# Token blocks of 512, split weights kept in DRAM, attention by pairs of heads, two element-wise steps as parametric ReLU on ScalarE

## The chip, the cores and the metric

One core of one Trainium2 chip. The metric is the device time of one execution in microseconds (us). Engines are named as in the profile: PE is TensorE's matmul side, PEld its weight loads, DVE VectorE, ACT ScalarE, POOL GpSimd, SP the SyncE queue that issues every DMA here.

## What is computed

Linear attention with random features over 4 batches of 8 heads, 576 tokens and 64 channels, and behind it two feed-forward layers on the 2304 tokens by 512 channels that come out of it:

```python
def phi(x):
    proj = np.einsum('bhsd,df->bhsf', x, w_phi)
    proj = proj - np.max(np.abs(proj), axis=-1, keepdims=True)
    return np.concatenate([np.exp(proj), np.exp(-proj)], axis=-1)
q_p, k_p = (phi(q), phi(k))
kv = np.einsum('bhsf,bhsd->bhfd', k_p, v)
z = np.sum(k_p, axis=2)
num = np.einsum('bhsf,bhfd->bhsd', q_p, kv)
den = np.einsum('bhsf,bhf->bhs', q_p, z)[..., None] + 1e-06
x = (num / den) laid out as 2304 x 512
h = x @ w_in;  x = np.maximum(0.01 * h, h) @ w_out     # layer 0, 512 -> 2048 -> 512
h = x @ w_in2; r = np.maximum(h, 0.0); out = (r * r) @ w_out2   # layer 1
```

The weights of the two layers are handed over as float64 words.

## The kernel before

**Split products.** Each float32 operand of the layers is split into a high part (rounded to float32r) and a low part (the rest, again float32r), and a product is three float32r matmuls: high x high, high x low, low x high. `copy` (line 256 on ACT, 258 on DVE) makes high parts, `sub` (line 261, DVE) low parts, so one line stands for many steps and the tiles' names tell them apart. All matmuls are issued at line 252.

**The two layers.** The hidden dimension is 16 chunks of 128. Layer 0 takes the tokens in 8 blocks of 288 (`HALF`), layer 1 in 6 blocks of 384 (`BLK2`). For a block and a chunk, `moe` issues the h part (12 matmuls, moving tiles `xh`, `xl` of the block against the chunk's `wih`, `wil`, into bank 74 or 75 in turn), the activation (`a` on ACT, `g` on DVE, high part `gh`, low part `gl`), and some chunks later the y part, which sums over the chunks in banks of its own. In layer 0 the activation is a copy scaled by 0.01 on ACT (L433) and a maximum on DVE (L441); in layer 1 a ReLU on ACT (L435) and a square on DVE (L443). Layer 0's y goes to DRAM (`x2d`), and layer 1 reads it back and splits it (`x2h`, `x2l`).

**The weights.** `w_fetch` loads a half chunk (w_in or w_out, 512 KB of float64 words, `raw`) and converts it: ACT scales the upper words (L347), DVE mends the sign (L352), shifts the lower words (L356) and joins both into `wf` (L361). Then `w_load` splits `wf` into the high and low part of one of 9 ring slots. The ring does not hold 16 chunks, so blocks go through the chunks forwards and backwards in turn; what must come again is kept as the 256 KB of `wf` in DRAM (`wsd`), and after each reload split again.

**Attention.** `k_pair` makes, for two heads, phi(k) and the sums over tokens (`kp`, `kvh`, `kvl`); `q_pair` makes phi(q) for two heads and 288 tokens (POOL's all-reduce for the maximum, `qm`, `qe`), the products, the reciprocal (L775), the product with it, and the block's `xh`, `xl`. Batch 0 is done in plain float32 (its matmuls show as two records each), batches 1 to 3 in split form (`qs`, `qeh`, `qel`). `i` counts the 8 stretches of 288 tokens, two per batch.

**The order.** A planner (`Plan.order`) gives every operation a position and a cost and writes one fixed order per engine; engines run their queues in that order. While it waits at the start, PE is given filler matmuls on a tile of zeros. SP's queue is in this order too, so a load that waits for a free buffer holds the ones behind it.

## Time and profile before

| | |
|---|---|
| three runs | 1041.18, 1042.75, 1045.9 us; median 1042.75 |
| the profiled execution | 1043.8 us, 1.8 above its span |
| its span | 1042.0 us |
| granted TensorE clock, mean | 0.987 |
| busy | PE 97%, PEld 92%, DVE 72%, ACT 58%, POOL 7% |
| DMA | 127.26 MB, mean 122 GB/s |

The span runs from the first instruction to the last. A matmul's recorded length overlaps the next one's, so PE's own pace is read from the starts of successive matmuls in a timeline, not from the mean length; for DVE and ACT the groups of instructions give a mean length each, and a window's busy time counts overlaps once.

### The profile page before, as it was taken

The numbers are of one execution on the slowest core, as the hardware profiler recorded it, in microseconds if no ns is written. First come the engines' busy times: TensorE is split into PE (matmuls) and PEld (weight loads), VectorE is DVE, ScalarE is ACT, GpSimd is POOL, SyncE is SP. The second block draws the span as 40 slices with busy tenths as digits, with TensorE's granted clock in tenths as the row PEclk, the third lists the DMA queues.
The fourth block names the chain that finished last, engine by engine and source line by source line (L and its number), as shares of the span: only waits on it lengthen the run. The fifth ranks groups of instructions, "written<-read, shape, count | busy, mean of one in ns | idle before, by whom it ended". The sixth has DMA issues, their size and how long they took to land.

```text
span 1042.0 us, 17543 instructions
## 1 busy us (share of the span) xinstructions
PE 1015.4 (97%) x6576; PEld 953.5 (92%) x6576; DVE 754.7 (72%) x1388; ACT 607.0 (58%) x1388; POOL 73.7 (7%) x37
## 2 busy tenths in 40 slices
PE   9986998999999999999999999999999999999998
PEld 7775998999999999999999999989999999999997
DVE  6999999988969989788896799985345263352442
ACT  5866777867657667567685566655344253342432
POOL 1210001111001110100110000000000000000000
PEclk9986999999999999999999999999999999999999
DMA  7577668413314314124032688875123032130300
GB/s 221 175 216 217 202 191 251 138 51 122 114 30 145 98 58 134 59 67 134 24 95 73 224 221 267 233 233 160 41 96 107 1 113 59 52 111 11 96 17 31
DMA packets 62566, 127.26 MB, mean 122 GB/s; under 512 B 6800, under 2 KB 15120, under 8 KB 62480
## 3 DMA queue, kind: packets, MB, share of 16 engines
q1 hardware_dynamic: 62480, 126.13, 40.0%
q8 instruction: 51, 0.84, 0.3%
q14 instruction: 35, 0.29, 0.1%
HBM read 101.99 MB, written 24.12 MB: 121 GB/s over the span
## 4 chain that ended last, share of the span: by engine, by line
PE 85%; DVE 7%; DMA 3%; ACT 3%; issue 1%; SPq 0%; DVEq 0%; ACTq 0%
PE bank L252 85%; DMA raw<-wd 2%; DVE wf L361 1%; DVE qden L775 1%; DVE raw L356 1%; DVE raw L352 1%; DVE wol L261 1%; DVE qs L261 1%; DMA x2d<-y 1%; DMA wsd<-wf 1%; DVE wil L261 0%; ACT raw L347 0%; DMA kt<-kd 0%; ACT qden L763 0%; DVE kmx L598 0%
## 5 line engine op out<-in xcount | busy, mean ns | idle before, releaser
L252 PE MATMUL bank<-xh,wih 128*128 128x288 f32 x512 | 153.3, 300 | 0.7 <-DVE g L441 0.3
L252 PE MATMUL bank<-xh,wil 128*128 128x288 f32 x512 | 151.4, 296 | 2.6 <-DVE wil L261 2.6
L261 DVE TENSOR_TENSOR gl<-g,gh 128x288 fp32r<-128x288 f32 (+1 forms) x224 | 115.1, 515 | 53.0 <-ACT gh L256 52.3
L256 ACT ACTIVATE gh<-g 128x288 fp32r<-128x288 f32 (+1 forms) x224 | 106.0, 475 | 80.4 <-DVE g L443 55.3
L252 PE MATMUL bank<-gh,woh 128*128 128x288 f32 x512 | 152.6, 298 | 0.0
L252 PE MATMUL bank<-gl,woh 128*128 128x288 f32 x512 | 151.3, 296 | 1.1 <-DVE gl L261 1.0
L252 PE MATMUL bank<-xl,wih 128*128 128x288 f32 x512 | 151.2, 295 | 0.0
L252 PE MATMUL bank<-gh,wol 128*128 128x288 f32 x512 | 150.7, 294 | 0.0
L252 PE MATMUL bank<-x2h,wil 128*128 128x384 f32 x384 | 130.1, 339 | 0.5 <-DVE wil L261 0.5
L252 PE MATMUL bank<-x2l,wih 128*128 128x384 f32 x384 | 130.5, 340 | 0.0
L252 PE MATMUL bank<-x2h,wih 128*128 128x384 f32 x384 | 129.1, 336 | 1.3 <-ACT wih L256 1.3
L252 PE MATMUL bank<-woh,gl 128*128 128x512 f32 x288 | 114.4, 397 | 0.0
L252 PE MATMUL bank<-wol,gh 128*128 128x512 f32 x288 | 114.0, 396 | 0.0
L443 DVE TENSOR_TENSOR g<-a 128x384 f32<-128x384 f32 x96 | 53.3, 555 | 83.4 <-ACT a L435 83.3
L252 PE MATMUL bank<-woh,gh 128*128 128x512 f32 x288 | 112.4, 390 | 0.1
L261 DVE TENSOR_TENSOR wol<-wf,woh 128x512 fp32r<-128x512 f32 x116 | 79.4, 686 | 42.3 <-ACT woh L256 41.7
L707 POOL PARTITION_ALL_REDUCE qm<-qps x32 | 73.2, 2287 | 478.5 <-ACT qps L256 236.0
L435 ACT ACTIVATE a<-bank 128x384 f32<-128x384 f32 x96 | 46.5, 484 | 96.2 <-PE bank L252 96.2
L256 ACT ACTIVATE woh<-wf 128x512 fp32r<-128x512 f32 x111 | 69.6, 628 | 52.2 <-PE bank L252 46.6
L252 PEld LDWEIGHTS bank<-xh,wil 128*128 128x128 f32 x512 | 96.6, 189 | 3.1 <-DVE wil L261 3.1
L252 PEld LDWEIGHTS bank<-xh,wih 128*128 128x128 f32 x512 | 96.8, 189 | 2.1 <-DVE g L441 1.3
L252 PEld LDWEIGHTS bank<-gl,woh 128*128 128x128 f32 x512 | 96.1, 188 | 2.0 <-DVE gl L261 1.7
(94 smaller groups left out, 2195.8 us busy)
## 6 DMA issues: line engine op xcount, KB each, us to landing
wf<-wsd SPq DMA_DIRECT2D x168, 256.0 KB, 2.8
raw<-wd SPq DMA_DIRECT2D x64, 512.0 KB, 4.6
wsd<-wf SPq DMA_DIRECT2D x56, 256.0 KB, 4.8
qt<-qd SPq DMA_DIRECT2D x32, 288.0 KB, 2.9
vt<-vd SPq DMA_DIRECT2D x16, 325.0 KB, 3.3
x2d<-y SPq DMA_DIRECT2D x32, 144.0 KB, 2.4
x2s<-x2d SPq DMA_DIRECT2D x6, 768.0 KB, 5.0
out<-o SPq DMA_DIRECT2D x18, 256.0 KB, 2.5
```

The source lines that it names most:

```text
L252: nc.tensor.matmul(out=o, lhsT=lhsT, rhs=rhs, start=start, stop=stop, **kw)
L256: nc.scalar.activation(out=out, in_=in_, func=ACTF.Copy)
L261: ENG[e].tensor_tensor(out=out, in0=a, in1=b, op=ALU.subtract)
L352: nc.vector.scalar_tensor_tensor(out=hf, in0=hf, scalar=2.0 ** 32, in1=hf, op0=ALU.mult, op1=ALU.min)
L356: nc.vector.tensor_scalar(out=low, in0=low, scalar1=29, scalar2=None, op0=ALU.logical_shift_right)
L361: nc.vector.scalar_tensor_tensor(out=t["f"].bitcast(I32), in0=high, scalar=3, in1=low, op0=ALU.logical_shift_left, op1=ALU.bitwise_or)
L435: nc.scalar.activation(out=t["a"], in_=o, func=ACTF.Relu)
L443: nc.vector.tensor_tensor(out=t["g"], in0=t["a"], in1=t["a"], op=ALU.mult)
L707: nc.gpsimd.partition_all_reduce(out_ap=t["m"].rearrange("p h s -> p (h s)"), in_ap=t["ps"].rearrange("p h s -> p (h s)"), channels=128, r ...
L775: nc.vector.reciprocal(out=t["d"], in_=t["d"])
```

## The change

- `BLOCKS`: both layers take the tokens in four blocks of 512 and one of 256. `xh` and `xl` come as tiles of 256 tokens, so an h part is 24 matmuls of 256 columns (one per tile and part); y of layer 0 moves 512 columns. Block 0 now needs the tokens 0 to 511, that is all four pairs of stretch i = 0 and of i = 1; block 1 needs the tokens 512 to 1023, up to the first 160 tokens of i = 3.
- The ring has 8 slots, and 5 more (`late`) from block 3 on, when attention's pools are closed. A chunk is split once. What must come again is stored as the slot itself, high and low part together (512 KB), and reloaded into a slot with no work on ACT or DVE.
- Layer 0's activation is one parametric ReLU on ACT (alpha 0.01). The sign step of the weights is folded into the scaling as a parametric ReLU with alpha 2^32.
- Attention's pieces are placed pair by pair: k of a pair and then both stretches of q of that pair.
- y of layer 1 uses banks 4 to 7 in each block, where before blocks took two sets of three banks in turn.
- Other positions, costs and buffer numbers in `P` and `tags`.

```diff
-NB1 = NT // HALF
-BLK2 = 384
+TILE = 256
+BLOCKS = [(0, 512), (512, 512), (1024, 512), (1536, 512), (2048, 256)]
...
-    ring=9, wf=6, raws=3,
+    ring=8, more=5, wf=2, raws=3,
...
-    wsd = dram.tile([2, NCH, 2, 128, DM], F32, name="wsd")
+    wsd = dram.tile([2, NCH, 2, 128, 2, DM], F32, name="wsd")
...
+        if (layer, c, half) in scratch:
+            load(
+                524288, pos - P["slead"], lambda: nc.sync.dma_start(out=slot(), in_=wsd[layer, c, half]),
+                w=[v], r=[scratch[layer, c, half]], after=gate,
+            )
+            return
...
-            nc.scalar.activation(out=hf, in_=hf, func=ACTF.Copy, scale=2.0 ** -112)
-
-        def sign(e):
-
-            hf = words()[1].bitcast(F32)
-            nc.vector.scalar_tensor_tensor(out=hf, in0=hf, scalar=2.0 ** 32, in1=hf, op0=ALU.mult, op1=ALU.min)
+            nc.scalar.activation(out=hf, in_=hf, func=ACTF.Prelu, scale=2.0 ** -112, alpha=2.0 ** 32)
...
+            for k in (k0, k0 + 1):
+                for m, (part, x) in enumerate(((0, "h"), (0, "l"), (1, "h"))):
+                    for u, (_, xs) in enumerate(xts):
+                        mm(
+                            o[:, u * TILE:(u + 1) * TILE], w_in(part, k), xs[x][:, k, :],
+                            k == 0 and m == 0 and u == 0, k == KD - 1 and m == 2, skip_group_check=True,
+                        )
...
+        def act_g(e):
+            t["g"] = new("g", [128, 512], F32)[:, :N]
+            nc.scalar.activation(out=t["g"], in_=banks[2 + n % 2][:, 0:N], func=ACTF.Prelu, alpha=0.01)
...
-            nc.scalar.activation(out=t["a"], in_=o, func=ACTF.Copy, scale=0.01)
...
-            nc.vector.tensor_tensor(out=t["g"], in0=o, in1=t["a"], op=ALU.max)
...
+    for b in range(B):
+        for p in range(PAIRS):
+            if b == 0:
+                tp = P["k0"] + P["kp0"] * p
+            else:
+                tp = at[NCH * (b - 1)] + P["kz"][b - 1] + P["kp"] * p
+            todo.append((tp - 12, 0, "k", (b, p, [tp + P["ks"] * o for o in range(5)])))
+            for c in range(2):
+                qp = tp + P["qk"] + P["qk2"] * c
+                todo.append((qp - 12, 1, "q", (qp, 2 * b + c, p)))
```

Three places show how the planner's order moves. The first is DVE where attention's last piece for block 1 of layer 0 is made (`xl<-qnum`, the low part of a piece of x). Before:

```order
L775 RECIPROCAL qden<-qden 128x288
L778 TENSOR_TENSOR qnum<-qnum,qden 128x288
L261 TENSOR_TENSOR wil_112<-wf,wih_111 128x512
L352 SCALAR_TENSOR_TENSOR raw<-raw 128x512
L261 TENSOR_TENSOR xl<-qnum,xh 128x288
```

And in the change:

```order
L791 RECIPROCAL qden<-qden 128x288
L794 TENSOR_TENSOR qnum<-qnum,qden 128x288
L263 TENSOR_TENSOR wo_102<-wf,wo_102 128x512
L260 CAST xh<-qnum 128x160
L263 TENSOR_TENSOR xl<-qnum,xh 128x160
L263 TENSOR_TENSOR gl<-g,gh 128x512
```

Before, 289 rows of DVE's order stand ahead of this `xl`, and now 345; the sign step (L352) is gone, and the last split of the first 16 chunks (`wo_102`) now stands just ahead.

The second is PE where block 1 of layer 0 begins (bank 75 is the last chunk of block 0, bank 74 the first of block 1). Before:

```order
L252 MATMUL bank_75<-xh,wih_111 128x288
L252 MATMUL bank_75<-xl,wih_111 128x288
L252 MATMUL bank_75<-xh,wil_112 128x288
L252 MATMUL bank_74<-xh,wih_111 128x288
L252 MATMUL bank_74<-xl,wih_111 128x288
```

And in the change, with a y part of an earlier chunk (banks 76, 77) in between:

```order
L254 MATMUL bank_75<-xh,wi_101 128x256 x4
L254 MATMUL bank_75<-xl,wi_101 128x256 x2
L254 MATMUL bank_75<-xh,wi_101 128x256 x2
L254 MATMUL bank_76<-gh,wo_98 128x512
L254 MATMUL bank_76<-gl,wo_98 128x512
L254 MATMUL bank_76<-gh,wo_98 128x512
L254 MATMUL bank_77<-gh,wo_98 128x512
L254 MATMUL bank_77<-gl,wo_98 128x512
L254 MATMUL bank_77<-gh,wo_98 128x512
L254 MATMUL bank_74<-xh,wi_101 128x256 x2
L254 MATMUL bank_74<-xl,wi_101 128x256 x2
```

Ahead of this first matmul of block 1 PE's order holds 16 chunks of 288 tokens before, and 16 chunks of 512 now.

The third is SP's queue in the stretch of reloads (`wsd` is the kept weights, `kt`, `krt`, `vt`, `qt` attention's inputs). Before, half chunks come into `wf`:

```order
L333 DMA wf<-wsd 128x512 x3
L551 DMA krt<-krd 64x128
L668 DMA qt<-qd 128x576
L333 DMA wf<-wsd 128x512 x9
L668 DMA qt<-qd 128x576
```

Now both parts come straight into the ring's slots:

```order
L344 DMA wi_101<-wsd 128x1024
L344 DMA wo_102<-wsd 128x1024
L344 DMA wi_99<-wsd 128x1024
L567 DMA krt<-krd 64x128
L563 DMA kt<-kd 128x512
L344 DMA wi_97<-wsd 128x1024
```

Over the whole program there were 168 such reloads of 256 KB and 56 stores of 256 KB; now there are 78 reloads of 512 KB and 44 stores of 512 KB.

## Rows read from the trace of the kernel before

**Rows 1.** Page, parts 1 and 4: busy time, and the chain's shares.

```profile
PE 1015.4 (97%) x6576; PEld 953.5 (92%) x6576; DVE 754.7 (72%) x1388; ACT 607.0 (58%) x1388; POOL 73.7 (7%) x37
...
PE 85%; DVE 7%; DMA 3%; ACT 3%; issue 1%; SPq 0%; DVEq 0%; ACTq 0%
```

**Rows 2.** Windows (length, then busy us and instructions per engine, PEclk, DMA share, GB/s).

```profile
78.00:104.00 26.00, 16.62 (x87) 15.26 (x88) 24.95 (x50) 16.64 (x39) 2.14 (x1) 0.67 0.75 217
...
0.00:168.60 168.60, 149.81 (x1066) 132.61 (x1067) 151.94 (x297) 116.60 (x287) 21.16 (x14) 0.93 0.69 205
168.60:1042.00 873.40, 865.56 (x5512) 820.89 (x5510) 602.73 (x1093) 490.39 (x1102) 52.53 (x23) 1.00 0.35 106
...
695.20:1038.40 343.20, 343.19 (x1708) 309.86 (x1708) 147.40 (x256) 135.96 (x261) 0.00 (x0) 1.00 0.23 70
```

**Rows 3.** Timeline of PE at block 1's start, and of DVE's `xl` ahead.

```profile
169.38 0.40 PE L252 MATMUL bank<-xh,wih 128*128 128x288 f32 x1
...
168.17 0.45 DVE L261 TENSOR_TENSOR xl<-qnum,xh 128x288 fp32r<-128x288 f32 x1
```

**Rows 4.** Groups on DVE up to 168.7 us (count | busy, mean ns | idle before).

```profile
L352 DVE SCALAR_TENSOR_TENSOR raw<-raw 128x512 f32<-128x512 f32 x32 | 24.3, 760 | 0.0
...
L441 DVE TENSOR_TENSOR g<-bank,a 128x288 f32<-128x288 f32 x14 | 6.3, 452 | 1.4 <-ACT a L433 1.4
```

**Rows 5.** Groups on DVE over the whole span, shapes kept apart.

```profile
L261 DVE TENSOR_TENSOR wol<-wf,woh 128x512 fp32r<-128x512 f32 x116 | 79.4, 686 | 42.3 <-ACT woh L256 41.7
L775 DVE RECIPROCAL qden<-qden 128x288 f32<-128x288 f32 x32 | 62.3, 1947 | 5.8 <-ACT qden L763 5.8
...
L261 DVE TENSOR_TENSOR qel<-qe,qeh 128x576 fp32r<-128x576 f32 x48 | 36.0, 752 | 0.9
L261 DVE TENSOR_TENSOR qs<-qt,qs 64x576 fp32r<-64x576 f32 x24 | 28.4, 1181 | 3.6 <-ACT qs L678 3.1
...
L258 DVE CAST qeh<-qe 128x576 fp32r<-128x576 f32 x16 | 7.3, 454 | 1.2 <-ACT qe L723 1.2
...
L599 DVE TENSOR_TENSOR ksb<-bank,kmx 128x128 f32<-128x128 f32 x16 | 4.7, 291 | 1.4 <-ACT kp L604 0.8
```

**Rows 6.** Groups on ACT over the whole span, shapes kept apart.

```profile
L433 ACT ACTIVATE a<-bank 128x288 f32<-128x288 f32 x128 | 51.8, 405 | 46.3 <-PE bank L252 45.4
L723 ACT ACTIVATE qe<-qm 128x288 f32<-128x288 f32 x128 | 48.0, 435 | 3.2 <-DVE qm L261 2.9 <-PE bank L252 0.2
L435 ACT ACTIVATE a<-bank 128x384 f32<-128x384 f32 x96 | 46.5, 484 | 96.2 <-PE bank L252 96.2
...
L347 ACT ACTIVATE raw<-raw 128x512 f32<-128x512 f32 x64 | 43.2, 675 | 15.5 <-DMA raw<-wd 15.1
```

**Rows 7.** Timeline of PE: starts of matmuls of 288, 256, 512 columns, and float32 ones.

```profile
497.55 0.29 PE L252 MATMUL bank<-xl,wih 128*128 128x288 f32 x1
...
498.61 0.28 PE L252 MATMUL bank<-wbh,kh 128*128 128x256 f32 x1
...
498.95 0.30 PE L252 MATMUL bank<-xh,wih 128*128 128x288 f32 x1
...
899.79 0.39 PE L252 MATMUL bank<-woh,gh 128*128 128x512 f32 x1
...
900.49 0.33 PE L252 MATMUL bank<-x2h,wih 128*128 128x384 f32 x1
...
20.85 1.90 PE L252 MATMUL bank<-vt,kp 128*128 128x65 f32 x16
22.68 0.49 PE L252 MATMUL bank<-wst,krt 64*128 64x128 f32 x2
```

**Rows 8.** The chain between the layers, in order of time.

```profile
682.97 5.21 DMA raw<-wd
...
695.12 4.97 PE bank L252 x17
```

**Rows 9.** Timeline: the last matmul.

```profile
1037.99 0.40 PE L252 MATMUL bank<-woh,gl 128*128 128x512 f32 x1
```

More of the change, by code (lines that the diff above doesn't have):

```diff
@@ L320, in attention_moe_moe, with w_load, slot @@
     w_val = {}
-    def w_fetch(layer, c, half, pos):
+    gate_late = []
+    def w_load(n, half, pos):
+        (layer, c), s = loads[n]
+        w_val[n, half] = v = Value(("ring", s, half))
+        gate = gate_late if s >= RING else []
+        def slot():
+            if s >= RING:
+                late()
+            return slots[s][half]
+        if (layer, c, half) in scratch:
[4 more added lines that the diff above has]
+            return
         raw, f = Value("raw"), Value("wf")
@@ L423, in moe @@
         before = [moe_h[n - 1]] if n else []
         cost = r_pass(N, 6)
-        plan.add(pe(cost), pos, lambda e: h_part(e, 0), r=[*xval, win], w=[hb], after=before)
-        moe_h[n] = plan.add(pe(cost), pos + 1, lambda e: h_part(e, 2), r=[*xval, win], w=[hb])
-        a, g, gh, gl = Value("a"), Value("g"), Value("gh"), Value("gl")
-        def act_a(e):
-            t["a"] = new("a", [128, BLK2], F32)[:, :N]
-            o = banks[2 + n % 2][:, 0:N]
-            if layer == 0:
-                nc.scalar.activation(out=t["a"], in_=o, func=ACTF.Copy, scale=0.01)
-            else:
-                nc.scalar.activation(out=t["a"], in_=o, func=ACTF.Relu)
@@ L437, in act_g @@
-        def act_g(e):
-            t["g"] = new("g", [128, BLK2], F32)[:, :N]
-            o = banks[2 + n % 2][:, 0:N]
-            if layer == 0:
-                nc.vector.tensor_tensor(out=t["g"], in0=o, in1=t["a"], op=ALU.max)
-            else:
-                nc.vector.tensor_tensor(out=t["g"], in0=t["a"], in1=t["a"], op=ALU.mult)
+        rd = [v for vs, _ in xts for v in vs]
+        plan.add(pe(cost), pos, lambda e: h_part(e, 0), r=[*rd, win], w=[hb], after=before)
+        moe_h[n] = plan.add(pe(cost), pos + N / HALF, lambda e: h_part(e, 2), r=[*rd, win], w=[hb])
@@ L808, in x2_block @@
-        lo, hi = i * BLK2 // HALF, ((i + 1) * BLK2 - 1) // HALF
-        load(786432, pos - 20, get, w=[xs], after=gate + [o for m in range(lo, hi + 1) for o in x2dep[m]])
-        for k in range(KD):
-            def h(e, k=k):
+            t["s"] = new("x2s", [128, KD, TILE], F32)
+            nc.sync.dma_start(out=t["s"], in_=x2d[:, :, k * TILE:(k + 1) * TILE])
+        i = next(i for i, (t0, N) in enumerate(BLOCKS) if t0 <= k * TILE < t0 + N)
+        pos = at[n1 + NCH * i] - P["xs"]
+        load(524288, pos - 20, get, w=[xs], after=gate_late + x2dep[i])
@@ L845, in attention_moe_moe @@
+            plan.add(to_lo(TILE), pos + d + 0.5, l, r=[xs], p=[xl], after=[a])
+        xv[1, k] = ([xh, xl], t)
     wq = list(plan_w)
```

304 lines of the change are left out of this document (138 added, 166 removed), and 6 rows, old and new, of the table tags.

## Prediction

> **What bounds the kernel now.** The busy shares and the chain [rows 1] say TensorE: 97% busy, 85% of the chain. Read by stretch [rows 2] there are two kernels. From 168.6 us to the end PE is busy 865.6 of 873.4 us; what counts there is PE's work and its pace. In the first 168.6 us it is not PE: DVE is busy 151.9 of 168.6, and from 78 to 104 us 24.95 of 26, while PE falls to 16.6 of 26 and the granted clock to a mean of 0.67 (so part of that stretch was spent at the lower level, 1.2 GHz, in between PE's waits). That stretch ends where block 1 of layer 0 starts: DVE makes the last low part of its x at 168.17, and block 1's first matmul starts at 169.38 [rows 3]. So the span is the time at which DVE has worked down its list for block 1, plus PE's work left from there, plus what PE loses on that way. Both sums can be made for the change, because its order is fixed.
>
> **PE's pace.** Start to start, eight matmuls of 288 columns take 1.06 us, 0.1325 each; three of 512 take 0.70, 0.233 each; three of 256 take 0.34, 0.113 each; a record of the float32 kind 1.83/16 = 0.114 [rows 7]. 288 and 512 columns cost 0.46 ns a column both; three matmuls are few, so for 256 I take the dearer end, 0.1173 (as 288, by column), and keep 0.113 for the range.
>
> First the check on the old kernel. From block 1's start its order has 1344 h and 1368 y matmuls of 288 columns in layer 0 (359.3 us), layer 1 with 96 chunks of 21 matmuls at 343.2 x 21/1708 = 4.22 [rows 2] (405.1) and attention: 288 records of `vt,kp` (0.114, 32.8), 380 split matmuls of 288 (50.4), 96 of 256 (11.3), 14 small ones (1.6). Sum 860.5; the clock from 169.38 to 1042.0 says 872.6. PE thus lost some 12 us there: 3.6 behind the last matmul's start, for the last copies and stores [rows 9], about 4 in the chain between the layers, where transfers of `raw` of 5.2 us are waited for [rows 8], and some 4.5 in small waits.
>
> **The change, part by part.**
>
> *PE's work from block 1 on.* Of 3648 matmuls of 256 columns 384 are done (block 0's h), of 1632 with 512 columns 162 (y of 13.5 chunks). Left: 3264 x 0.1173 = 382.9, 1470 x 0.233 = 342.5, attention 288 records x 0.114, 192 + 64 split matmuls x 0.1325, 96 x 0.1173 and 16 small ones x 0.114, 80 together. Sum 805. The whole work of the layers is not changed by the new blocks (same columns, 0.46 ns each); PE simply has 55 us less of it left at this point, since block 0 is 512 tokens now instead of 288.
>
> *DVE's list up to block 1's last low part.* Successive DVE instructions overlap by some 0.05 us, so I take each 0.05 under its mean; with this the old list's 297 instructions add up to 152.1, against 151.94 measured [rows 2]. Gone: 32 sign steps x 0.70 (0.760 [rows 4]) = 22.3 and 14 maxima x 0.40 = 5.7. Added, because four more pairs of batch 0 and four of batch 1 must be through: 8 reciprocals x 1.89 = 15.2, 16 `qel` x 0.70 = 11.2, 7 `qs` x 1.13 = 7.9, 10 `qeh` casts x 0.40 = 4.0 [rows 5], 8 subtractions of `qm` at `qel`'s length = 5.6, 8 products 3.4, 14 `gl` of 512 columns x 0.63 (the 686 ns row of that size) in place of 14 of 288, 3.3; 31 pieces of `xl` of 32 to 256 columns in place of 8: the nearest row is a 128-column subtraction at 291 ns, so 0.24 to 0.40 each, 4 to 9 more, I take 5; casts of x, splits and copies 7. Sum -28 + 63 = +35, so 187 us.
>
> *DVE's idle time on that way.* Before it was 168.6 - 151.9 = 16.7. Much of this is the start, which does not change. But ACT is now nearly as loaded: to its 116.6 busy us come 40 exponentials (0.385 each net), 49 copies out of PSUM for q (0.355), 16 for k, 17 splits (0.63) and 20 activations and high parts of 512 columns for 29 of 288, so about 178 where DVE has 187. Two engines that wait for each other at 85 to 90% idle more: lower bound 16.7, upper bound 33 (a DVE at 85%). I take 25. Block 1 starts at 187 + 25 + 1 = 213.
>
> *The parametric ReLU.* No row shows one. Copy with a scale takes 675 ns for 512 columns, ReLU 484 for 384, exponential 435 for 288 [rows 6]: length sets the time, not the function, so I price it as the copy it replaces, at nothing extra; were it twice that, 32 x 0.68 = 22 us more on ACT, and ACT would be the later one (second rival). VectorE's share of the work moves to ScalarE here, and the trace says this is the right way round: up to block 1 DVE, not ACT, is the engine that is waited for. The Trainium skill speaks against it ("ScalarE: Activation LUTs", Rules for kernel authors: for relu, max and min use VectorE, not ScalarE). By that rule the 28 us would stay on DVE's list and the sum would end 28 us later, past the old time; no row here bears the rule out, and the way in which it could still be right is the second rival.
>
> *The reloads.* 168 splits after a reload go away (high on ACT, low on DVE, 0.63 each, some 105 us of DVE), nearly all of it after block 1, where DVE was busy 602.7 of 873.4 [rows 2] beside a PE that was full. Its cover was PE, so I cost it at nothing directly. What it buys is fewer small waits: DVE's list after block 1 falls to about 380 us beside 812, so of the 4.5 us of small waits I keep 3. Bytes hardly change (168 x 256 KB become 78 x 512 KB). In SP's queue reloads no longer wait for a `wf` buffer but for a slot; the last y of the chunk that held it is long done when blocks turn round.
>
> *Between the layers.* The same 32 half chunks are converted, now with 13 slots and without the sign step; the 4 us wait shrinks or stays: 2.
>
> *The end.* One copy and store less behind the last matmul, otherwise as before: 3.6.
>
> **Sum.** 213 + 805 + 3 + 2 + 3.6 = 1026.6 span, against 1042.0. The profiled execution lay 1.8 above its span and the median of the runs 1.05 below that execution, so 1027 as a median, 1.5% under 1042.75.
>
> **The rivals.**
>
> *More is gained (below 1014).* DVE idles no more than before (16.7), PE loses 1 us in small waits, 256 columns cost 0.113 (3264 x 0.0043 = 14 less): 205 + 791 + 1 + 5.6 = 1003; with the first two alone 1017. For it: the new order puts few weights ahead of block 0. Against it: the load on ACT. 0.12.
>
> *ACT takes DVE's place at the start (1038 to 1060).* ACT idled 52 of the first 168.6 us [rows 2]. If its waits for PE and DVE stay what they were, it is through with its 178 us at 230, block 1 starts there, and the span is 230 + 805 + 8.6 = 1044: no change. Beyond some 55 us of idle time it is a loss. For it: DVE, ACT and PE pass the work of one pair to each other, with little conversion work now to fill the gaps, and all of batch 0 stands ahead of block 0. Against it: ACT's waits were mostly for the DVE that now has less per pair to do beside. 0.20, of which 0.13 end within 0.5%.
>
> *Weight loads set the pace (slower).* Each weight load shows 188 ns while matmuls of 288 columns start every 132: loads already overlap, PEld is busy 92% of the span [rows 1], and the kernel now loads twice as often per h column. If in a long stream a matmul of 256 columns still took the 0.1325 of a 288 one, the 3648 of them would cost 55 us more: 1082. The change loses from 0.1173 + 16/3648 = 0.122 on. Against it: three in a row went at 0.113, and float32 records of 65 columns, which have little to stream, start every 0.114, so a load can be had in that time. A rule of the Trainium skill would have this rival ("Trainium Kernel Development and Optimization", Performance Expectations: the busy share of LDWEIGHTS, not of matmuls, tells how near TensorE is to its limit). The rows do not follow it so far: the share is 92% while the pace is set by columns. 0.07.
>
> What else could go wrong (a load that holds SP's queue in block 0, where 32 `raw` loads and some 22 stores of 512 KB and 8 MB of attention, 36 MB, must pass in the 200 us before the last conversion: 180 GB/s, and 205 were moved before [rows 2]) gets 0.03, two thirds of it slower.
>
> **How the numbers follow.** My forecast, 1014 to 1037, has 0.58. A measurement of this kernel can tell about 0.5% from no change (1037.5 to 1048). Faster: 0.58 + 0.12 = 0.70. Within: 0.13 + 0.01 = 0.14. Slower: 0.07 + 0.07 + 0.02 = 0.16. The range for 8 in 10 takes in most of the better case (down to 1006, where 1003 is its end) and the second rival up to where it is no change (1047).
>
> **What would show it.** In the new profile: block 1's first h matmul at 205 to 221 us, and DVE busy 183 to 191 us before it (an earlier start with the same work means less idle time; a later one with ACT above 88% busy means the second rival). First h matmul of block 0 near 80 us. Start to start in a long stream of h matmuls 0.113 to 0.118 per matmul; 0.122 or more is the third rival. ACT's parametric ReLUs near 0.67 us (512 columns in place) and 0.59 (out of PSUM), and one table load. After block 1 PE busy all but 15 us. The forecast is wrong in kind, not in size, if PE loses over 20 us after block 1, or if DVE has been done with block 1's x long before PE gets to it.

## The result, and the profile after

The changed kernel takes 1034.26 us (median of four runs, 1033.95 to 1034.82); the kernel before, run beside it, 1043.68 (four runs, 1041.18 to 1045.9). The ratio is 0.9916, with a 95% interval of 0.9888 to 0.9945: faster, by 0.8%, where 1.5% was forecast. The profiled execution has a span of 1032.2 us (forecast 1026.6) and a mean granted clock of 0.997.

The page's parts 1 and 4, as [rows 1] of before:

```profile
PE 1011.3 (98%) x6689; PEld 915.6 (89%) x6689; DVE 583.3 (57%) x1060; ACT 472.6 (46%) x1056; POOL 73.0 (7%) x37
...
PE 77%; DVE 17%; ACT 4%; issue 2%; DVEq 0%; POOL 0%; ACTq 0%; POOLq 0%
```

TensorE is busy 98%, VectorE fell from 72% to 57% and ScalarE from 58% to 46%; in the chain VectorE's share rose from 7% to 17%. Windows of the new profile (columns as in [rows 2]), the same first stretch as there, then cut where block 0 of layer 0 (79.82 us) and block 1 (206.83 us) start, and at 452 us:

```profile
78.00:104.00 26.00, 23.75 (x163) 22.56 (x164) 24.30 (x47) 18.45 (x44) 2.73 (x2) 0.89 0.62 208
79.82:206.83 127.01, 122.10 (x817) 111.08 (x817) 122.84 (x218) 95.91 (x221) 16.32 (x7) 0.99 0.71 236
0.00:206.83 206.83, 195.46 (x1299) 168.55 (x1300) 188.55 (x351) 154.69 (x385) 36.40 (x21) 0.98 0.65 212
206.83:452.00 245.17, 239.33 (x1633) 219.54 (x1632) 179.51 (x320) 137.45 (x332) 32.31 (x14) 1.00 0.39 128
206.83:1032.20 825.37, 815.81 (x5391) 747.05 (x5389) 394.76 (x710) 317.87 (x672) 36.59 (x16) 1.00 0.32 107
```

From 78 to 104 us TensorE is busy 23.75 us at a mean clock of 0.89, where it was 16.62 at 0.67. Up to block 1 VectorE is busy 188.55 us and idle 18.3; behind it TensorE is busy 815.81 of 825.37 us. Where block 1 starts, on TensorE and VectorE, as [rows 3]:

```profile
206.83 0.40 PE L254 MATMUL bank<-xh,wi 128*128 128x256 f32 x2
...
207.49 0.33 DVE L263 TENSOR_TENSOR xl<-qnum,xh 128x160 fp32r<-128x160 f32 x1
```

Block 1's first h matmul starts at 206.83 without a wait. The last `xl` of block 1 is begun only at 207.49, in time for the second half of that h part. So TensorE's own work, and not only the end of VectorE's list, stands right ahead of this start. In a long stretch of layer 1 TensorE's starts are, as [rows 7]:

```profile
900.75 0.64 PE L254 MATMUL bank<-xh,wi 128*128 128x256 f32 x4
901.24 0.40 PE L254 MATMUL bank<-xl,wi 128*128 128x256 f32 x2
901.48 0.40 PE L254 MATMUL bank<-xh,wi 128*128 128x256 f32 x2
```

Four matmuls of 256 columns take 0.49 us here, two 0.24: 0.120 to 0.122 each, where 0.1173 was taken. ScalarE's groups, shapes kept apart, with the parametric ReLUs of the weights (L365) and of layer 0 (L447), as [rows 6]:

```profile
L365 ACT ACTIVATE raw<-raw 128x512 f32<-128x512 f32 x64 | 42.4, 671 | 1.5 <-DMA raw<-wd 1.4
...
L447 ACT ACTIVATE g<-bank 128x512 f32<-128x512 f32 x64 | 38.0, 593 | 82.5 <-PE bank L254 82.2
...
L258 ACT ACT_TABLE_LOAD x1 | 1.3, 1283 | 0.7 <-PEq L922 0.7
```

And the end of the chain, as [rows 8, 9]: from 443.35 us on it is TensorE without a break, through the change of layers, up to the last copies and stores.

```profile
443.35 585.15 PE bank L254 x3822
```

### The profile page after: what moved, and what is told of

It reads as the page before. It is cut to its first block, busy times and chain, and to the rows that moved or that the text cites. A ratio compares the mean times of both kernels' runs of the same rounds, so it can differ in the third digit from the quotient of the medians.

```text
span 1032.2 us, 16724 instructions
## 1 busy us (share of the span) xinstructions
PE 1011.3 (98%) x6689; PEld 915.6 (89%) x6689; DVE 583.3 (57%) x1060; ACT 472.6 (46%) x1056; POOL 73.0 (7%) x37
## 4 chain that ended last, share of the span: by engine, by line
PE 77%; DVE 17%; ACT 4%; issue 2%; DVEq 0%; POOL 0%; ACTq 0%; POOLq 0%
PE bank L254 77%; DVE qden L791 2%; DVE qel L263 2%; DVE qs L263 2%; DVE gl L263 1%; DVE qm L263 1%; DVE wf L374 1%; DVE ksb L615 1%; DVE qeh L260 1%; DVE qnum L794 1%; DVE raw L369 1%; DVE kmx L614 1%; DVE xl L263 1%; ACT qe L737 1%; ACT qden L777 1%
## 5 line engine op out<-in xcount | busy, mean ns | idle before, releaser
L254 PE MATMUL bank<-xh,wi 128*128 128x256 f32 x2304 | 422.1, 284 | 0.3 <-DVE wi L263 0.3
L254 PEld LDWEIGHTS bank<-xh,wi 128*128 128x128 f32 x2304 | 355.2, 191 | 17.1 <-DVE wi L263 0.5
L254 PE MATMUL bank<-xl,wi 128*128 128x256 f32 x1152 | 243.0, 283 | 0.0
L254 PE MATMUL bank<-gh,wo 128*128 128x512 f32 (+1 forms) x640 | 206.5, 374 | 0.0
L254 PEld LDWEIGHTS bank<-xl,wi 128*128 128x128 f32 x1152 | 183.9, 191 | 1.0
L263 DVE TENSOR_TENSOR gl<-g,gh 128x512 fp32r<-128x512 f32 (+1 forms) x160 | 102.6, 641 | 142.4 <-ACT gh L258 140.9
L254 PE MATMUL bank<-wo,gh 128*128 128x512 f32 x576 | 180.8, 395 | 0.0
L254 PEld LDWEIGHTS bank<-gh,wo 128*128 128x128 f32 x640 | 117.4, 189 | 17.9
L254 PE MATMUL bank<-gl,wo 128*128 128x512 f32 (+1 forms) x320 | 118.9, 372 | 0.0
L254 PE MATMUL bank<-wo,gl 128*128 128x512 f32 x288 | 112.0, 389 | 0.0
L447 ACT ACTIVATE g<-bank 128x512 f32<-128x512 f32 (+1 forms) x80 | 44.0, 550 | 91.3 <-PE bank L254 85.7
```

The lines of the kernel that those rows point to most:

```text
L254: nc.tensor.matmul(out=o, lhsT=lhsT, rhs=rhs, start=start, stop=stop, **kw)
L263: ENG[e].tensor_tensor(out=out, in0=a, in1=b, op=ALU.subtract)
L447: nc.scalar.activation(out=t["g"], in_=banks[2 + n % 2][:, 0:N], func=ACTF.Prelu, alpha=0.01)
```

## The experiments

Two sums serve below. One is where block 1 of layer 0 starts (before 169.38, after 206.83). The other is what TensorE does from there: busy and not busy. Each run's numbers come from its own windows, cut at its own start of block 1.

### What a matmul of 256 columns costs

A kernel of its own, with streams of one width each (one execution):

```diff
+    def stream(bank, shapes, reps):
+        for _ in range(reps):
+            for c, w in shapes:
+                nc.tensor.matmul(out=banks[bank][:, 0:w], lhsT=st[:, c * 128:(c + 1) * 128], rhs=mv[:, 0:w], ...)
...
+    stream(5, each(256), 32)
```

> This kernel leaves the whole computation out and only runs streams of 96 to 128 float32r matmuls, one width after the other: 64, 128, 192, 224, 256, 288, 384 and 512 columns with four weight blocks in turn, then 256 columns where each weight block is used twice in a row, then a cycle of one matmul of 512 and three of 256 columns. Read is the time from start to start. Theory A, a weight load sets a floor in a long stream: 64 to 256 columns all start about every 0.120 us (the pitch of the 256-column h matmuls in the changed kernel), 288 every 0.1325, 512 every 0.233, and the cycle of 512 and three 256 takes 0.573 (0.233 + 3 x 0.113, the loads run ahead behind the long one). Theory B, 256 columns themselves take 0.120 (a fixed part per matmul on top of 0.46 ns a column): 128 columns near 0.06, 64 near 0.035, 192 near 0.09, and the cycle 0.593 (0.233 + 3 x 0.120). By A 224 columns cost as much as 256; by B 0.015 less.

Groups of TensorE by width, then windows: one in the stream of 128 columns, at a granted clock of 0.50, and then a short and a long one each, at 1.00, within the streams of 256, of 512, of 256 with each weight block twice, and of the cycle of one 512 and three 256. The count in a window has the matmuls at its edges in it, so the pace is read from the difference of two:

```profile
L217 PE MATMUL bank<-mv,st 128*128 128x384 f32 x128 | 22.4, 334 | 0.0
L217 PE MATMUL bank<-mv,st 128*128 128x288 f32 x128 | 17.0, 294 | 0.0
...
L217 PE MATMUL bank<-mv,st 128*128 128x224 f32 x128 | 14.5, 275 | 0.0
```

```profile
60.00:75.00 15.00, 15.00 (x72) 15.00 (x72) 0.00 (x0) 0.00 (x0) 0.00 (x0) 0.50 0.01 1
111.00:113.00 2.00, 2.00 (x19) 2.00 (x19) 0.00 (x0) 0.00 (x0) 0.00 (x0) 1.00 0.00 0
111.00:125.00 14.00, 14.00 (x119) 14.00 (x119) 0.00 (x0) 0.00 (x0) 0.00 (x0) 1.00 0.00 1
167.00:169.00 2.00, 2.00 (x11) 1.65 (x10) 0.00 (x0) 0.00 (x0) 0.00 (x0) 1.00 0.00 0
167.00:191.00 24.00, 24.00 (x108) 19.88 (x107) 0.00 (x0) 0.00 (x0) 0.00 (x0) 1.00 0.00 1
196.00:198.00 2.00, 2.00 (x19) 2.00 (x19) 0.00 (x0) 0.00 (x0) 0.00 (x0) 1.00 0.00 0
196.00:208.00 12.00, 12.00 (x102) 12.00 (x102) 0.00 (x0) 0.00 (x0) 0.00 (x0) 1.00 0.01 1
211.00:213.00 2.00, 2.00 (x16) 1.86 (x16) 0.00 (x0) 0.00 (x0) 0.00 (x0) 1.00 0.00 0
211.00:226.00 15.00, 15.00 (x104) 13.83 (x104) 0.00 (x0) 0.00 (x0) 0.00 (x0) 1.00 0.00 0
```

A group's busy time counts overlaps once, so 128 matmuls of 288 columns give (17.0 - 0.29)/127 = 0.132 us each, 384 columns (22.4 - 0.33)/127 = 0.174, 224 columns (14.5 - 0.28)/127 = 0.112. The windows give 12/100 = 0.120 for 256 columns, 22/97 = 0.227 for 512, and the same 0.120 (10/83) with the weights used twice in a row. 192 columns, at 1.00 too, are no cheaper than 224 (80 more matmuls between 84 and 95 us than between 84 and 86, 0.1125 each), and neither are 64 columns in the first microseconds of their stream, where the clock was still 1.00 (18 more between 29 and 32 us than between 29 and 30, 0.111 each). The widths from 256 to 512 lie near one line: 0.107 us for 256 columns more, that is 0.417 ns a column, and 0.0133 us a matmul besides. Below it there is a floor of 0.112. So 256 columns are just above the floor: theory B holds for them, but not for fewer columns, and A's floor exists, but lower than A put it. The cycle takes 4 x 13/88 = 0.591, as B had it (0.593).

### h in matmuls of 512 columns

x in a ring of contiguous pieces, so that one matmul takes both, first in six blocks of 512, then in all eight:

```diff
-                    for u, (_, xs) in enumerate(xts):
-                        mm(o[:, u * TILE:(u + 1) * TILE], w_in(part, k), xs[x][:, k, :], ...)
+                    step = TILE if s0 + N // TILE > 5 else N
+                    for u in range(0, N, step):
+                        c = (s0 * TILE + u) % (5 * TILE)
+                        mm(o[:, u:u + step], w_in(part, k), xr[x][k][:, c:c + step], ...)
```

> The change with one edit: x stands in a ring of five contiguous pieces of 256 tokens, so that in six of the eight blocks of 512 tokens an h part is 12 matmuls of 512 columns and not 24 of 256; in the two blocks whose pieces wrap round the ring (block 2 of layer 0, block 0 of layer 1) it stays as it was. Order and costs of the planner are unchanged. Theory (the mis-sized term is the pitch of 256-column matmuls, 0.120 where the forecast took 0.1173): a chunk's h falls from 24 x 0.120 = 2.88 to 12 x 0.233 = 2.80, 0.084 less; 80 such chunks lie behind block 1's start, so the span falls by 6.7 us to 1025.5, a time of 1027.5. Rival (the 0.120 comes from waits between matmuls that have nothing to do with their width, or PE is not what sets the pace): within 2 us of the changed kernel's 1034.3, and 512-column h matmuls at 0.240.

Measured: 1020.06 us, ratio 0.9776 (0.9748 to 0.9804), span 1017.9. It is 14.3 us of span less, twice the forecast of 6.7. The window behind block 1's start, and layer 1's matmuls in a timeline:

```profile
206.16:1017.90 811.74, 801.20 (x4431) 696.59 (x4429) 395.25 (x710) 318.24 (x672) 36.62 (x16) 1.00 0.32 109
```

```profile
900.01 0.62 PE L255 MATMUL bank<-xh,wi 128*128 128x512 f32 x2
900.46 0.39 PE L255 MATMUL bank<-xl,wi 128*128 128x512 f32 x1
...
900.91 0.61 PE L255 MATMUL bank<-wo,gh 128*128 128x512 f32 x2
901.37 0.39 PE L255 MATMUL bank<-wo,gl 128*128 128x512 f32 x1
```

Now every matmul of 512 columns, of h and of y alike, takes 0.227: from 900.01 to 901.37 there are six, one of them an `xh` at 900.69. The forecast had taken 0.233, the pace of y matmuls that stand beside other widths. So a chunk's h falls by 24 x 0.120 - 12 x 0.227 = 0.156, 12.5 us in 80 chunks, and the y matmuls, cheaper by some ns too, can make up the rest.

```diff
+                    if turned(layer, i):
+                        mv = xr[x][k].rearrange("p (s c) -> p s c", s=5)[:, 0:5:4, :]
+                    else:
+                        mv = xr[x][k][:, c:c + N]
+                    mm(o[:, 0:N], w_in(part, k), mv, ...)
```

> As the run with 512-column h matmuls, now in all eight blocks of 512 tokens: where the two pieces of x wrap round the ring, one matmul takes them as two pieces of 256 in the order in which they stand, and the block's stores put the halves of tokens back in their order (layer 0's y with two stores, layer 1's by rows). Theory (a matmul costs one column per 0.4167 ns and 0.0133 us besides, so halving their number pays 0.0133 for each one saved, and a column's time does not depend on whether the moving operand is contiguous): 32 chunks x 12 x 0.0133 = 5.1 us less than in that run, all behind block 1's start: span 1012.8, time 1015. Rival (two pieces in one moving operand cost what two matmuls do): no difference, 1020.

Measured: 1016.5 us, ratio 0.9742 (0.97 to 0.9784), span 1016.1. This is the fastest kernel of the study, 17.8 us under the change by the medians.

```profile
0.00:207.56 207.56, 195.24 (x1107) 157.92 (x1108) 188.21 (x351) 154.37 (x384) 36.42 (x21) 0.98 0.63 210
207.56:1016.10 808.54, 797.58 (x4047) 677.45 (x4045) 394.72 (x711) 318.23 (x672) 36.60 (x16) 1.00 0.33 110
238.00:243.00 5.00, 4.04 (x16) 3.62 (x16) 2.07 (x3) 2.82 (x7) 0.00 (x0) 0.66 0.96 353
```

Behind block 1's start TensorE needs 808.5 us where the run before needed 811.7: 3.2 less of the 5.1 expected. Part of the rest lies in this one execution: in the second of two waits, of 0.65 and 0.96 us, its granted clock fell to 0.50 near 239 us for some 3.4 us (mean 0.66 from 238 to 243). The spans of the four executions lie between 1013.1 and 1016.1 us, this one's being the longest, where 1012.8 was expected. In layer 1's first block, whose operand lies in two pieces, the starts are:

```profile
680.72 0.62 PE L255 MATMUL bank<-xh,wi 128*128 128x512 f32 x2
681.17 0.39 PE L255 MATMUL bank<-xl,wi 128*128 128x512 f32 x1
```

Two matmuls take 0.45 us, as with one piece. A moving operand in two pieces costs what one piece does. Block 1 itself started 1.4 us later in this execution, which the runs do not explain.

### Is it VectorE's list that sets block 1's start?

Work was added to VectorE, added to ScalarE, and taken off VectorE, each with everything else in its place. The sign step back on VectorE:

```diff
-            nc.scalar.activation(out=hf, in_=hf, func=ACTF.Prelu, scale=2.0 ** -112, alpha=2.0 ** 32)
+            nc.scalar.activation(out=hf, in_=hf, func=ACTF.Copy, scale=2.0 ** -112)
...
+            nc.vector.scalar_tensor_tensor(out=hf, in0=hf, scalar=2.0 ** 32, in1=hf, op0=ALU.mult, op1=ALU.min)
```

> The change with the sign step of the weights back on VectorE: ScalarE scales by a copy, VectorE mends the sign just before it joins the words; every other operation stays where it was in each engine's order. Theory (VectorE's list sets block 1's start): 32 more steps of 0.70 us lie ahead of block 1, so it starts 18 to 22 us later than 206.8, at 225 to 229, VectorE's idle time up to there stays near 18, and since 32 further steps behind block 1 lie beside a full TensorE, the time is 1052 to 1057. Rival (ScalarE, or the chain that the engines pass each other, sets it): VectorE takes up its idle time, block 1 starts less than 10 us later and the time is under 1045.

Measured: 1055.13 us, ratio 1.0115 (1.0073 to 1.0157). Up to block 1, and behind it:

```profile
0.00:224.50 224.50, 199.52 (x1299) 168.89 (x1300) 207.38 (x381) 155.77 (x384) 35.34 (x21) 0.98 0.60 198
224.50:1053.50 829.00, 817.52 (x5391) 746.98 (x5389) 415.32 (x744) 317.31 (x672) 36.62 (x16) 1.00 0.32 106
```

VectorE is busy 18.8 us longer, block 1 starts 17.7 later, and VectorE's idle time stays near 17 (17.1, 18.3 in the change). Ahead of block 1 this added work counts nearly in full.

A second ScalarE pass behind each parametric ReLU of the weights:

```diff
             nc.scalar.activation(out=hf, in_=hf, func=ACTF.Prelu, scale=2.0 ** -112, alpha=2.0 ** 32)
+            nc.scalar.activation(out=hf, in_=hf, func=ACTF.Copy, scale=1.0)
```

> The change with each parametric ReLU of the weights followed by a second ScalarE pass over the same words (a copy by 1.0, in place), all else in its place: 64 passes of 0.62 us net, 32 of them ahead of block 1, so 20 us more on ScalarE there, where it is busy 154.7 of 206.8. Theory (VectorE's list sets block 1's start, ScalarE has the room): it starts at most 8 us later, the time is 1034 to 1042. Rival (ScalarE stands in the chain of each pair in turn with VectorE, so that its work counts in full, the second rival of the prediction): 15 to 20 us later, 1049 to 1055.

Measured: 1046.24 us, ratio 1.0022 (0.9997 to 1.0047), 12 us over the change by the medians, 8.8 by the spans.

```profile
0.00:212.43 212.43, 195.72 (x1299) 168.49 (x1300) 189.44 (x351) 175.08 (x417) 36.11 (x21) 0.98 0.63 207
```

20.4 us more on ScalarE move block 1 by 5.6, and another 3 us went behind block 1's start. The start is within the theory's 8, but the median time lies between the theory's 1042 and the rival's 1049. The profiled execution took 1042.75 us, 3.5 less than the median of the ten, so these windows do not show the whole cost.

Work taken off VectorE, by leaving out the low words of the weights:

```diff
         def shift(e):
-            low = words()[0]
-            nc.vector.tensor_scalar(out=low, in0=low, scalar1=29, scalar2=None, op0=ALU.logical_shift_right)
+            return
...
-            nc.vector.scalar_tensor_tensor(
-                out=t["f"].bitcast(I32), in0=high, scalar=3, in1=low, op0=ALU.logical_shift_left, op1=ALU.bitwise_or
-            )
+            nc.vector.tensor_scalar(out=t["f"].bitcast(I32), in0=high, scalar1=3, scalar2=None, op0=ALU.logical_shift_left)
```

> The change with work taken off VectorE: the low words of the weights are left out (the shift of the low words goes away, and the join becomes a shift of the high words alone), so the weights are cut behind 20 bits and the output is that of cut weights; all else is in its place. Ahead of block 1 that is 32 x 0.40 (shift) and some 32 x 0.25 (the join's length falls from 0.70 net to that of a one-operand shift), about 21 us of VectorE's 188.6. Theory of the prediction (VectorE's list alone sets block 1's start): it starts 17 to 21 us earlier, at 186 to 190, the time is 1013 to 1018. Rival (in the order as it is TensorE itself is as full: from block 0's first h at 79.8 to 206.8 us it is busy 122.1 of 127.0, so what VectorE gives free it can use only for those 4.9 us and a part of its waits ahead of 79.8): block 1 starts 4 to 9 us earlier, VectorE's idle time up to there rises from 18 to 30 or more, and the time is 1025 to 1030.

Measured: 1028.07 us, ratio 0.9851 (0.981 to 0.9892).

```profile
0.00:200.44 200.44, 193.57 (x1300) 168.87 (x1300) 170.69 (x319) 154.75 (x386) 35.56 (x21) 0.98 0.67 218
```

VectorE is relieved of 17.9 us, and block 1 starts only 6.4 earlier. VectorE's idle time grows from 18.3 to 29.7 us, TensorE's falls from 11.4 to 6.9. The rival holds: in this order TensorE and VectorE are both full ahead of block 1, and relief of one soon meets the other.

The old kernel with the parametric ReLUs alone (the tile `a`, which now is `g` too, gets a third buffer):

```diff
-            nc.scalar.activation(out=hf, in_=hf, func=ACTF.Copy, scale=2.0 ** -112)
+            nc.scalar.activation(out=hf, in_=hf, func=ACTF.Prelu, scale=2.0 ** -112, alpha=2.0 ** 32)
...
-                nc.scalar.activation(out=t["a"], in_=o, func=ACTF.Copy, scale=0.01)
+                nc.scalar.activation(out=t["a"], in_=o, func=ACTF.Prelu, alpha=0.01)
...
-                nc.vector.tensor_tensor(out=t["g"], in0=o, in1=t["a"], op=ALU.max)
+                t["g"] = t["a"]
```

> The kernel before with one part of the change alone: both parametric ReLUs (sign step of the weights, and leaky ReLU), every operation left in its place in the old order, the 64 sign steps and 128 maxima of VectorE simply gone. Theory (VectorE's list sets block 1's start): 32 x 0.70 + 14 x 0.40 = 28 us less ahead of block 1 of layer 0; VectorE idles about 17 as before (a little more, since ScalarE is busy 116.7 of then only 145), so block 1 starts at 141 to 148 where it started at 169.4, TensorE's way from there is unchanged, and the time falls from 1042.5 to 1014 to 1021. Rival (other engines or TensorE's own chain of attention stand close behind): less than 14 us earlier, over 1029. Under the theory this part alone brings more than the whole change did (8 us), so the other parts together cost 13 to 20.

Measured: 1034.13 us, ratio 0.9912 (0.9884 to 0.994). The theory is out by 13 us and more. The kernel before from 104 us to its block 1, then this run up to its block 1, from 78 to 104 us, and behind its block 1's start:

```profile
104.00:169.38 65.38, 62.04 (x455) 58.73 (x453) 62.26 (x125) 45.83 (x107) 2.52 (x1) 1.00 0.69 203
```

```profile
0.00:167.27 167.27, 153.22 (x1070) 135.38 (x1071) 130.42 (x252) 115.15 (x288) 21.38 (x14) 0.93 0.68 207
78.00:104.00 26.00, 18.46 (x94) 16.98 (x94) 21.86 (x42) 17.24 (x41) 2.14 (x1) 0.67 0.74 226
167.27:1033.10 865.83, 861.29 (x5508) 818.71 (x5506) 545.71 (x945) 487.66 (x1102) 51.67 (x23) 1.00 0.35 107
```

VectorE's busy time falls by 22 us (152.7 to 130.4) and block 1 starts 2.1 us earlier, at 167.27; VectorE idles 36.9 us now. From 104 us on TensorE was busy 62.04 of 65.38 us in the old kernel already, so there was next to nothing to win there. Most of this run's gain came where the theory had none: behind block 1's start TensorE takes 865.8 us for 872.6, 6.8 of the 8.9 us of span. Part of it lies at the change of layers, where TensorE in the old kernel waited 1.29 us for the first weights of layer 1 and from 690 to 699 us had a mean clock of 0.81; neither shows in this run. From 78 to 104 us, where TensorE did have room, it is busy 18.46 us, hardly more than the 16.62 of [rows 2], and the clock is the same 0.67. TensorE's own waits there still end in VectorE's `ksb` (7.0 us, 8.6 in the old kernel). ScalarE waits longer for the loads of `raw` (3.2 us there, 1.7 in the old kernel), so VectorE's queue may now stand behind ScalarE and the loads; that is not shown.

### What the parametric ReLU is worth in the new order

Both undone, then layer 0's step alone. The edit of layer 0's step (the sign step's stands above):

```diff
-            nc.scalar.activation(out=t["g"], in_=banks[2 + n % 2][:, 0:N], func=ACTF.Prelu, alpha=0.01)
+            nc.scalar.activation(out=t["g"], in_=banks[2 + n % 2][:, 0:N], func=ACTF.Copy, scale=0.01)
+            nc.vector.tensor_tensor(out=t["g"], in0=banks[2 + n % 2][:, 0:N], in1=t["g"], op=ALU.max)
```

> The change without either parametric ReLU: the sign step and the leaky ReLU are done as before, a copy on ScalarE and a second step on VectorE, all in their place in the changed order. With the run in which only the sign step was undone (block 1 at 224.5, VectorE busy 207.4 and idle 17.1 up to there) 14 to 16 maxima of 0.64 net come to VectorE's list, 9 to 10 us. Theory (work added to a full VectorE counts in full): block 1 at 232 to 235, the time 1062 to 1067; the other parts of the change (blocks, kept weights, order) would then lose 20 to 25 us against the kernel before by themselves, and the parametric ReLUs be worth some 30 in the new order where they were worth 8 in the old. Rival (the maxima fall into VectorE's waits for ScalarE): block 1 under 229, the time under 1060.

Both undone, measured: 1083.85 us, ratio 1.0389 (1.0337 to 1.044).

> The change with the leaky ReLU alone undone: ScalarE copies with the factor 0.01, VectorE takes the maximum, in place; the sign step stays a parametric ReLU. The sign step alone cost 21 us over the change, both together 49.6 (30 ahead of block 1, the rest behind). Theory A (the costs add: the maximum also puts one more hop between engines into the chain from an h part to its y part, and a bank comes free only behind it): 25 to 30 us over the change, 1059 to 1064, a part of it behind block 1's start. Theory B (VectorE is pushed over its limit only with both): the 14 to 16 maxima ahead of block 1 cost 8 to 12 us, behind it next to nothing, 1042 to 1048.

Layer 0's alone, measured: 1059.4 us, ratio 1.0128 (1.0061 to 1.0195). A window behind block 1 of the run with both undone, then windows up to block 1 and behind it of the run with layer 0's step undone:

```profile
234.53:1081.80 847.27, 821.50 (x5391) 747.16 (x5389) 448.62 (x809) 316.37 (x672) 36.64 (x16) 1.00 0.32 104
```

```profile
0.00:218.18 218.18, 199.02 (x1300) 169.44 (x1300) 195.97 (x366) 156.13 (x385) 36.62 (x21) 0.98 0.63 203
218.18:1057.30 839.12, 819.82 (x5391) 747.25 (x5389) 428.14 (x775) 318.50 (x672) 36.62 (x16) 1.00 0.32 105
```

With both undone, block 1 starts at 234.53, as expected, but the time is 17 us above the theory's 1067: behind it TensorE is idle 25.8 us (847.27 - 821.50) where the change has 9.6, and busy 5.7 more. So of the 49.6 us of span 27.7 come ahead of block 1 and 21.9 behind it. Layer 0's step alone costs 25.1 (11.4 ahead, 13.7 behind), the sign step alone 21.3 (17.7 and 3.6): they add up, nearly, as theory A had it. Behind block 1, where I took VectorE's work as covered, the sign step came back with 3.6 us of the 20.6 that VectorE was busy longer there, layer 0's step with 13.7 of 33.4 (428.14 - 394.76). What TensorE waits for in the 273 us from block 1's start, nearly all of it beside attention, in the change and then with layer 0's step undone:

```profile
PE bank L254 <- DVE ksb L615: 2.5, 4, 0.8
PE bank L254 <- ACT qden L777: 1.6, 4, 0.9
...
PE bank L254 <- DVE ksb L616: 6.2, 9, 1.7
PE bank L254 <- ACT qden L778: 5.3, 7, 1.2
```

The waits that grow end in attention's pieces, and none there ends in the maximum, so theory A's longer chain from h to y is not what these waits show. The two steps also stand in different places: 29 of the maxima lie between block 1's start and 480 us, beside attention, and only 2 of the sign steps; the other 30 lie behind 599 us, where attention is over. Ahead of block 1, too, layer 0's step cost more (11.4) than VectorE's list grew by it (195.97 - 188.55 = 7.4). Whether place or chain makes the difference is not told apart.

Taken together: both parametric ReLUs are worth 8 us in the old order and 50 in the new, and the rest of the change, without them, loses 42 us against the kernel before.

### The reloads

```diff
+            a = plan.add(to_hi(DM), pos - 0.5, again_h, p=[v], after=[a])
+            plan.add(to_lo(DM, True), pos - 0.4, again_l, p=[v], after=[a])
             return
```

> The change with the element-wise work of the reloads put back: after each of the 78 reloads of 512 KB both parts are written again in place (ScalarE or VectorE copies the high part, VectorE goes over the low part at a subtraction's length); the planner knows these steps and orders them. All lie behind block 1's start. Theory (a full TensorE covers them): 78 x 0.63 = 49 us more on VectorE, which is busy 395 of 825 us there, and as much on ScalarE: the time is within 3 us of the changed kernel's 1034.3. Rival (the cover is gone where attention stands beside layer 0, from 207 to 445 us, with VectorE busy 177 of 238): TensorE idles 5 us or more longer behind block 1's start, 1040 and above.

Measured: 1037.83 us, ratio 0.9955 (0.9935 to 0.9974), 3.6 over the change by the medians, 3.8 by the spans: a hair beyond the theory's 3, and below the rival's 1040.

```profile
207.04:1036.00 828.96, 816.60 (x5391) 747.00 (x5389) 441.78 (x785) 356.81 (x753) 36.19 (x16) 1.00 0.32 107
```

VectorE has 47 us more and ScalarE 39 behind block 1, and TensorE's time there grows from 825.37 to 828.96. TensorE idles 2.8 us longer, under the rival's 5. Sparing these 78 pairs of steps is worth some 4 us here; the old kernel had 168 smaller reloads, and that number was not tried.

### Two attempts on the fastest kernel

The subtraction of the maximum to GpSimd, behind its all-reduce, and VectorE's early casts to ScalarE:

```diff
-        plan.add(to_lo(576), pos + D8[2], lambda e: sub(e, t["m"], t["ps"], t["m"]), r=[ps], w=[qm])
+        plan.add(to_lo(576), pos + D8[2], lambda e: sub("POOL", t["m"], t["ps"], t["m"]), r=[ps], w=[qm])
```

> The kernel with 512-column h matmuls in all blocks, and one step of attention, the subtraction of the maximum (qm, 128 x 576), taken from VectorE to GpSimd, just behind the all-reduce that it follows there; all else in its place. Theory (VectorE's list sets block 1's start): 16 x 0.70 = 11 us less on VectorE ahead of block 1, GpSimd is busy only 36 of 207 us there, so block 1 starts 8 to 11 us earlier than without the edit and the time is 1004 to 1007. Rival (the step takes so much longer on GpSimd, or slows VectorE so much, that the pair's chain through qm and the exponentials gets longer by as much): no gain, 1013 or more.

Measured: 1306.55 us, ratio 1.2517 (1.2463 to 1.2571). GpSimd's timeline from its first all-reduce on:

```profile
11.94 2.16 POOL L741 PARTITION_ALL_REDUCE qm<-qps  x1 [10.91 <-ACT qps L259]
21.26 1.39 POOL L264 TENSOR_TENSOR qm<-qps,qm 128x576 f32<-128x576 f32 x1 [7.16 <-issue]
28.55 2.15 POOL L741 PARTITION_ALL_REDUCE qm<-qps  x1 [5.90 <-issue]
```

The subtraction itself takes 1.39 us. But ahead of it GpSimd stands 7.16 us with nothing that the profile shows to wait for, and 5.90 ahead of an all-reduce that follows a subtraction. Over the run all 32 subtractions have such a gap ahead, of 6.7 to 9.3 us, and no all-reduce behind a subtraction starts less than 5.7 us after it. One all-reduce and one subtraction thus hold GpSimd for 16.6 us (11.94 to 28.55). In the chain that ended last "issue" has 20% of 1301.6 us, 260 us, most of the 290 lost. The time lies in the rival's direction, but neither theory had these gaps.

```diff
-        if e == "ACT":
+        if e == "ACT" or early[0]:
```

> The kernel with 512-column h matmuls in all blocks, with the 44 casts and copies that VectorE did ahead of block 1 (10 qeh, 16 pieces out of the sums, 8 q, 10 of x, k and weights; 17 us busy) on ScalarE, in the same places. Theory by the runs so far (18 us less on VectorE brought 6.4, 20 us more on ScalarE cost 5.6; TensorE is nearly full itself): about 15 less on VectorE and 20 to 24 more on ScalarE cancel, block 1 starts within 4 us of 207.6, the time stays at 1013 to 1020. Rival (VectorE's list alone counts and ScalarE has 53 us of room): 10 us earlier or more, under 1008. Other rival (ScalarE's waits in its fixed order then hold the chain up): 1024 or more.

Measured: 1018.37 us, ratio 0.9736 (0.9691 to 0.9781).

```profile
0.00:207.78 207.78, 194.32 (x1108) 156.61 (x1109) 173.61 (x303) 170.50 (x432) 35.89 (x21) 0.99 0.64 213
```

The casts and copies go to ScalarE until block 1's first h is issued. 14.6 us less on VectorE (188.2 in the kernel without the edit) and 16.1 more on ScalarE (154.4 there): block 1 at 207.78, as in the kernel without the edit. The first theory holds, and ScalarE's 53 us of idle time are no free room.

## Why the prediction was right, and where its steps were off

**In sum.** The likeliest case came, inside its range of 1014 to 1037, but with little over half the gain: 1034.3 where 1027 was named. Block 0's first h matmul came at 79.82 (forecast near 80). On the profiled spans the miss is 5.6 us, the net of two: block 1 started 6.2 us earlier than forecast (206.8 for 213), and TensorE took 11.8 longer from there (825.4 for 813.6).

**VectorE's list: right.** 188.55 us measured up to block 1, 187 forecast. **Its idle time: off by 6.7**, 18.3 and not 25; it lay near the lower bound. ScalarE, busy 154.7 us and not 178 by then, was not nearly as loaded as I made it: up to block 1 its exponentials for q are 32 more than before, not 40, and its instructions for `kp` and `kvf` none more, where 16 copies for k were priced.

**The pace of 256 columns: the mis-sized term.** The forecast took 0.1173, scaled by columns from 288; measured are 0.120. 3264 x 0.0027 = 8.8 of the 10.8 us that TensorE was busy longer. What failed is "288 and 512 columns cost 0.46 ns a column both": that was read from three y matmuls of 512 at 0.233, a little dear beside other widths. By the streams a matmul pays 0.0133 us besides its columns, so narrow matmuls cost more for the same columns: in the streams 288 columns take 0.132 us, 384 take 0.174 and 512 take 0.227. By these prices the layers' matmuls (before 3072 of 288, 1152 of 384 and 864 of 512 columns, now 3648 of 256 and 1632 of 512) come to some 6 us more than before, an estimate. "The whole work of the layers is not changed" falls with it. The third rival came in small, 0.120 against the 0.122 from which the change would have lost. Its floor is there, but at 0.112, below what 256 columns take. Whether the fixed part belongs to the weight load that each matmul has of its own is not told apart: in the stream that uses each weight block twice there are as many loads.

The Trainium skill ("Trainium Kernel Development and Optimization", Performance Expectations) counts the busy share of the weight loads among the good measures of how close a kernel is to its roofline. The kernel with wide h matmuls everywhere is faster with a share of 82%, where the change has 89%; the traces do not bear the rule out for that share.

**Waits behind block 1: right.** TensorE idles 9.6 us there, where 8.6 was the sum of three terms. Some of it moved: 5.8 us fall to attention up to 452 us, none is left between the layers (2 forecast), 3.7 come later, the end among them.

**The parametric ReLU: right in price.** 671 ns for 512 columns in place, 593 out of the sums, one table load (0.67 and 0.59 forecast). In place it takes what the copy with a scale took [rows 6]. The Trainium skill ("ScalarE: Activation LUTs", Rules for kernel authors) would have such steps on VectorE. The measurement decides against it here: on VectorE they cost 21 us (the sign), 25 (layer 0's) and 50 (both).

**The reloads: right.** Costed at nothing; measured, 86 us of element-wise work beside 78 reloads come to under 4 us.

**The reading of the old start: wrong.** "In the first 168.6 us it is not PE" averaged two stretches. From 104 us on TensorE was as full as VectorE (62.04 of 65.38 us), so the end of VectorE's list beside block 1's start was no proof that it set it. The run with the parametric ReLUs alone in the old order shows this: 22 us less on VectorE, 2 earlier. In the change both engines are full up to block 1 (from 79.82 us on TensorE is busy 122.10 of 127.01 us): there the sign step's additions count nearly in full (17.7 of 18.8), reductions by a third (6.4 of 17.9). A sum over VectorE's list alone could not know that TensorE's own work ends at the same time, so that it came within 6 us of block 1's start is in part luck.

**Where the gain came from.** From 78 to 104 us TensorE was busy 7.1 us longer than before, at a mean clock of 0.89 for 0.67. The clock has a part in this. Windows of the old kernel:

```profile
84.50:101.50 17.00, 9.63 (x41) 9.14 (x42) 16.76 (x33) 10.22 (x23) 1.77 (x1) 0.50 0.78 234
690.00:699.00 9.00, 7.16 (x28) 5.95 (x27) 5.73 (x11) 3.22 (x7) 0.00 (x0) 0.81 0.74 250
```

In the old kernel waits of 2.26, 1.78 and 4.53 us for `ksb` lie between 83 and 97 us, and its clock was 0.50 from 84.5 to 101.5, where a matmul of 288 columns took 0.24 us for 0.1325; it fell again for some 3.4 us behind the wait between the layers. The change has neither stretch (0.99 from 79.82 us to block 1, 1.00 behind). Its TensorE is busy 4.1 us less in all (1015.4 to 1011.3) although its matmuls of 256 columns are dearer, and idle 5.7 us less. How much of the 9.8 us of span the clock makes up is not told apart. Without the parametric ReLUs the new order is 42 us slower than the old kernel, so the gain is theirs and the order's together. Whether it is the longer block 0 that gives TensorE work there, beside the conversions, is not shown: no run varied the length of block 0 alone, and a first block of 256 tokens was not tried.

**The second rival** did not come: ScalarE idles 52 us up to block 1, and its added work counted by a quarter (5.6 of 20.4, in the profiled execution).

## What to carry to other kernels

Before a stretch is put down to one engine, cut it where the busy shares change, and look whether a second engine is as full: here, where two were, added work on one cost in full and saved work was mostly not returned. Price a matmul by the pace of a long stream of its own width, and issue the widest that the operands allow. Fold element-wise steps between two matmuls into the pass that reads the sums: beside attention such a step was not hidden here, though VectorE was busy only 179.51 of 245.17 us.
